# A softmax maximum per partition in a two-layer decode kernel: exp with a maximum, partial maxima joined per head, and q's copies on another engine

## The chip, the cores and the metric

The kernel runs on one core of a Trainium2 chip. A core has five engines that run side by side, each taking its own instructions in program order: TensorE (PE in the profile, its weight loads PEld), VectorE (DVE), ScalarE (ACT), GpSimd (POOL) and SyncE (SP). They meet at semaphores. Data comes from device memory (HBM) by DMA into SBUF, 128 partitions wide; matmuls write PSUM, 8 banks of 128 x 512 fp32. The metric is the device time of one execution in microseconds, lower is better. Before the change it is 1034.55 us, the median of three runs (1034.34 to 1034.6).

## The reference

Two pairs of layers on x of shape 8 x 1 x 448 in bf16. Layer A is grouped-query attention over a cache of 4096 positions, 16 query heads on 8 key/value heads of 256; layer B is a small MLP (with one position its shifted parts vanish, since they read only padding). Both pairs use the same weights and the same cache, so that the second pass reads the same K and V again.

```python
def _A_ref(x, k_cache, v_cache, wq, wo):
    q = (x @ wq).reshape(B, Sq, Hq, Dh).transpose(0, 2, 1, 3)
    k = jnp.repeat(k_cache, rep, axis=1)
    v = jnp.repeat(v_cache, rep, axis=1)
    scores = jnp.einsum("bhqd,bhkd->bhqk", q, k) * (Dh ** -0.5)
    p = jax.nn.softmax(scores, axis=-1)
    o = jnp.einsum("bhqk,bhkd->bhqd", p, v)
    return o.transpose(0, 2, 1, 3).reshape(B, Sq, Hq * Dh) @ wo

x = x + _A_ref(_layernorm(x), k_cache, v_cache, wq, wo)
x = x + _B_ref(_layernorm(x), w1, w2, w3, w4)
x = x + _A_ref(_layernorm(x), k_cache, v_cache, wq, wo)
x = x + _B_ref(_layernorm(x), w1, w2, w3, w4)
```

K and V have 8 x 8 x 4096 x 256 values each, 134 MB in bf16: 268 MB for one pass over both.

## The kernel before

**Units and tiles.** The work is cut into 64 units: pass (`ps`, 0 or 1), batch row (`b`, 0 to 7) and group pair (`gp`, 0 to 3, two key/value heads, hence four query heads). A unit has four K tiles and four V tiles of 1 MB, which lie in 17 places (`slots`, `places`) in SBUF. To save transfers, for each row 14 of the 16 tiles of group pairs 2 and 3 (called kept, and two more in part, in `rest` and in PSUM banks `store`) stay in place from pass 0 to pass 1. `free` units are those of group pairs 0 and 1.

**Order.** The list `items` fixes, ahead of time, in which order K and V tiles of which units are worked on; the loop at L1266 goes through it and issues every engine's instructions. The middle of the program is made of rounds, one per batch row. A round begins with K tiles of five units (V tiles of older units between them), and ends with the V tiles of three free units, which are read in halves (`narrow`, `halved`), while the rest of the layers for this row (wo, MLP, q of pass 1: the generator `chain`, moved on by `step`) and the kept K tiles of pass 1 go through. In that last part 14 places hold kept tiles, so that three places are left to turn over.

**Loads.** `emit_loads` issues the next transfers of the fixed order on SP's queue as soon as the program has given up a place (L920 for K, mostly two tiles at once; L931 to L937 for V). SP waits there until the place's last reader is done, and everything behind it waits with it.

**K side.** A K tile is transposed in place by DVE in 32 x 32 blocks (L1003): one instruction over 2048 words for the first tile of a pair, three (1024, 512, 512) for the second. Then PE computes the scores of the pair (`scores`, L1018), 32 matmuls of 128 x 256, with the query laid out block-diagonally in `qbd` as weights. They land in bank `sc`, on 8 of each 32 partitions: four blocks `k` of positions, in each of them four chunks by two heads. `qbd` is filled by `spread_q`: four small matmuls (L409) into `misc` and four copies by DVE (L415). ACT makes P from the scores (`exps`, L1027, one per pair): exp without a maximum, with the sum of each partition as second output in `z_t`; the profile shows an extra instruction that reads this accumulator.

**P and V.** Between the halves of the next scores, `turn_p` turns the unit's P by four matmuls with an identity (L1069) into `misc`, and ACT casts it into one of five buffers `psv` (L1076). Per V tile ACT copies the tile's part into `ptw` (L1261), and PE multiplies (`pv`, L1086) into `o`.

**After a unit.** `half` (L555) takes o out of PSUM by ACT (L546), multiplies it with R by fp32 matmuls (L592), which turns it and divides it by the sums. R is `rz` times a 0/1 pattern `fold` (L575). `rz` comes from `z_cols` (L512): DVE adds the two partial sums per partition (L518), spreads them by head with the pattern `usel` (L521), PE adds over partitions with a matrix of ones (L529), DVE takes the reciprocal (L532).

Of the kernel before, what the change touches and what calls it, by code (L numbers as in the profile page):

```python
# [17 lines left out]
def kernel(  # L18
# [79 lines left out]
    usel = consts.tile([128, 4], FP32, name="usel")  # L98
    for u in range(2):
        nc.vector.tensor_reduce(  # L100
            usel[:, 2 * u : 2 * u + 2],
            ident.rearrange("p (k q h) -> p h k q", k=4, h=2)[:, :, :, 2 * u : 2 * u + 2],
            mybir.AxisListType.XY,
            ALU.add,
        )

    parity = consts.tile([128, 2], FP32, name="parity")
    nc.vector.tensor_reduce(
        parity[:], ident.rearrange("p (m k) -> p k m", k=2), mybir.AxisListType.X, ALU.add
# [16 lines left out]
        psv_t[:, 128 * k : 128 * k + 128].rearrange("p (a n h) -> p a n h", a=4, h=2)  # L126
# [24 lines left out]
    wv = consts.tile([128, 4], FP32, name="wv")  # L151
# [3 lines left out]
    one = consts.tile([128, 1], FP32, name="one")  # L155
    nc.vector.memset(one[:], 1.0)
    ones = one[:].to_broadcast([128, 128])
# [6 lines left out]
    eps2 = consts.tile([128, 2], FP32, name="eps2")  # L164
    nc.vector.memset(eps2[:, 0:1], EPS)
    nc.vector.memset(eps2[:, 1:2], EPS * EPS / (1 + EPS))
    nhalf = consts.tile([128, 1], FP32, name="nhalf")
    nc.vector.memset(nhalf[:], -0.5)
# [66 lines left out]
    def norm(x, nb, twice, xe=None):  # L235
# [18 lines left out]
        nc.vector.tensor_mul(xx[:, 0], x, wv[:].unsqueeze(2).to_broadcast([128, 4, nb]))  # L254
# [39 lines left out]
        def power(k0, k1):  # L294
# [3 lines left out]
                nhalf[:].to_broadcast([128, (k1 - k0) * nb]),  # L298
# [3 lines left out]
        if twice and nb == 1:  # L302
            nc.vector.scalar_tensor_tensor(
                ve[:, :, 0], var.to_broadcast([128, 2]), 0.0, eps2[:], ALU.max, ALU.add
# [44 lines left out]
    def project_q(b):  # L349
# [10 lines left out]
        nc.vector.tensor_copy(OT2[:, :, HH:, b], q_ps.rearrange("p (j h) -> p j h", j=2))  # L360
        yield

    def project_rows(w_of, h0, hn, r0, r1, ps, cols=None):
# [14 lines left out]
        for j in range(2):  # L378
            nc.vector.tensor_copy(
                OT2[:, j, h0 : h0 + hn, r0:r1],  # L380
                ps[:, j * hn * nb : (j + 1) * hn * nb].rearrange("p (h b) -> p h b", b=nb),
            )

    def tail_cols(r0, r1, ps, two):
# [10 lines left out]
            parity[:].unsqueeze(2).to_broadcast([128, 2, nb]),  # L395
# [4 lines left out]
    def spread_q(b, h0, ng, qbd):  # L400
# [12 lines left out]
        for a in range(4):  # L413
            u = a // 2
            nc.vector.tensor_copy(  # L415
# [96 lines left out]
    def z_cols(zall, gps):  # L512

        np_ = len(gps)
        zm = chn.tile([128, 4, np_], FP32, tag=f"zm{np_}")
        zs_t = chn.tile([128, 2], FP32, tag="zs")
        zs = zs_t[:, 0:np_]
        nc.vector.tensor_add(  # L518
# [747 lines left out]
    for idx, it in enumerate(items):  # L1266
# [53 lines left out]
        elif kv == 0:  # L1320
# [19 lines left out]
            if c == 3 and q_begun:  # L1340
                run(q_begun.pop())
# [286 lines left out]
```

## Time and profile before

| | |
|---|---|
| median of three runs | 1034.55 us (1034.34 to 1034.6) |
| the profiled execution | 1035.43 us, its span 1033.2 us |
| mean granted TensorE clock | 0.656 |
| HBM read | 419.63 MB, 406 GB/s over the span |
| DVE: transposes of K (L1003) | 444.0 us in 384 instructions |
| PE: P times V (L1086) | 245.6 us in 3808 matmuls |
| PE: scores (L1018) | 234.8 us in 4736 matmuls |
| ACT: exp (L1027) | 95.3 us in 128 instructions, and 33.9 us for reading the accumulator |
| ACT: copies into ptw (L1261) | 52.7 us in 248 |
| DVE: q's copies (L415) | 30.8 us in 184, 61.7 us idle before them |
| DVE: reciprocals of the sums (L532) | 9.5 us in 55 |

The span is the time from the first to the last instruction; the execution's own time is 2.2 us longer. "Busy" is time in which an engine executes; waiting at a semaphore does not count. "Idle before" is an engine's idle time directly before the instructions of a group, followed by what ended most of it. The DMA share is that of the core's 16 DMA engines, which all queues share. The page's digits for 40 slices of the span show the rounds: every fourth slice or so DVE falls from 9 to 2 tenths, while DMA stays at 9 everywhere but in the last slice.

### The profile page before, as it was taken

How to read it: one execution, taken by the hardware profiler on the slowest of the kernel's cores; microseconds unless marked ns; L12 is line 12 of the kernel's file. 1: busy time of each engine (PE TensorE's matmuls, PEld its weight loads, DVE VectorE, ACT ScalarE, POOL GpSimd, SP SyncE). 2: the span in 40 equal slices, each digit the busy share in tenths (PEclk: the TensorE clock that was granted, in tenths of full speed). 3: DMA queues.
4: the chain of work that ended last, by engine and by line, in shares of the span. 5: the costliest groups of instructions: out<-in, count | busy, mean ns of one | idle time of the engine just before them, and what ended most of it. 6: DMA issues, size and time to landing. Idle time of an engine off the chain costs nothing.

```text
span 1033.2 us, 28609 instructions
## 1 busy us (share of the span) xinstructions
PE 657.3 (64%) x12707; PEld 415.6 (40%) x12707; DVE 585.8 (57%) x1213; ACT 212.7 (21%) x688; POOL 16.3 (2%) x27
## 2 busy tenths in 40 slices
PE   3154445876587557865784577558865874577775
PEld 2022222443245334533452345334533552345544
DVE  6334567159725961587249725872497259624581
ACT  1011111141214120412141214121412141214110
POOL 0000000000000000000000000000000000000000
PEclk9999855576557665566656667655565566656655
DMA  9999999999999999999999999999999999999995
GB/s 365 389 426 421 422 424 419 388 425 423 415 404 412 425 416 402 400 424 417 408 419 424 418 394 413 423 418 406 420 422 412 407 418 423 417 396 409 415 422 216
DMA packets 69290, 421.48 MB, mean 408 GB/s; under 512 B 7080, under 2 KB 12976, under 8 KB 43568
## 3 DMA queue, kind: packets, MB, share of 16 engines
q1 hardware_dynamic: 69120, 419.66, 99.1%
q8 instruction: 99, 1.62, 0.6%
q14 instruction: 23, 0.19, 0.0%
q10 hardware_dynamic: 48, 0.01, 0.0%
HBM read 419.63 MB, written 0.01 MB: 406 GB/s over the span
## 4 chain that ended last, share of the span: by engine, by line
DMA 48%; DVE 23%; PE 20%; issue 3%; SPq 3%; ACT 2%; POOL 0%; DVEq 0%; ACTq 0%
DMA places<-in_A_v_cache_dram 31%; DVE places L1003 18%; DMA places<-in_A_k_cache_dram 16%; PE sc L1018 9%; PE o L1086 5%; PE misc L180 2%; PE misc L592 2%; ACT p_n L1027 1%; DVE qbd L415 1%; DVE store L1049 1%; DMA places<-in_A_wq_dram 1%; SPq L934 1%; SPq L199 1%; PE misc L529 1%; PE misc L453 1%
## 5 line engine op out<-in xcount | busy, mean ns | idle before, releaser
L1003 DVE STREAM_TRANSPOSE places<-places 128x512 uint32<-128x512 uint32 (+2 forms) x384 | 444.0, 1213 | 44.3 <-DMA places<-in_A_k_cache_dram 43.8
L1086 PE MATMUL o<-places,ptw 128*8 128x256 bf16 x3808 | 245.6, 381 | 140.7 <-DMA places<-in_A_v_cache_dram 112.6
L1018 PE MATMUL sc<-places,qbd 128*8 128x256 bf16 (+1 forms) x4736 | 234.8, 353 | 149.2 <-DVE places L1003 148.7
L1018 PEld LDWEIGHTS <-qbd 128*8 128x8 bf16 x4736 | 122.4, 104 | 216.7 <-DVE places L1003 124.8
L1086 PEld LDWEIGHTS <-ptw 128*8 128x8 bf16 x3968 | 102.0, 101 | 205.7 <-issue 128.7
L1027 ACT ACTIVATE p_n<-sc 128x256 bf16<-128x256 f32 x128 | 95.3, 744 | 330.8 <-PE sc L1018 328.5
L1261 ACT COPY ptw<-psv 128x32 bf16<-128x32 bf16 x248 | 52.7, 227 | 179.7 <-PE o L1086 178.1
L415 DVE CAST qbd<-misc 32x16 bf16<-32x16 f32 (+1 forms) x184 | 30.8, 167 | 61.7 <-PE misc L409 59.9
L592 PE MATMUL misc<-R_t,o_t 128*128 128x4 f32 (+1 forms) x212 | 45.7, 322 | 29.1 <-DVE qbd L415 12.6
L592 PEld LDWEIGHTS misc<-R_t,o_t 128*128 128x128 f32 x212 | 41.4, 272 | 45.0 <-issue 18.7
L1076 ACT CAST psv<-misc 128x128 bf16<-128x128 f32 x64 | 17.0, 265 | 196.8 <-PE misc L1069 196.8
L532 DVE RECIPROCAL rz<-misc 128x4 f32<-128x4 f32 (+1 forms) x55 | 9.5, 172 | 80.1 <-PE misc L529 36.1
L1054 ACT COPY places<-store 128x1024 bf16<-128x1024 bf16 x40 | 40.2, 1030 | 10.6 <-PE o L1086 10.3
L529 PE MATMUL misc<-zm,one 128*128 128x4 f32 (+1 forms) x110 | 27.1, 317 | 18.4 <-DVE zm L521 16.0
L529 PEld LDWEIGHTS misc<-zm,one 128*128 128x128 f32 x110 | 22.3, 253 | 34.0 <-DVE zm L521 22.8
L180 PEld LDWEIGHTS <-w_sb 128*128 128x128 bf16 x896 | 27.8, 105 | 16.7 <-issue 16.7
L1027 ACT ACTIVATION_READ_ACCUMULATOR p_n<-sc 128x1 f32 x128 | 33.9, 265 | 0.0
L546 ACT COPY o_t<-o 128x256 f32<-128x256 f32 x53 | 19.7, 372 | 56.4 <-PE o L1086 56.3
L295 POOL TENSOR_TENSOR t<-t,nhalf 128x2 f32<-128x2 f32 (+2 forms) x18 | 12.0, 669 | 953.5 <-DVE t L316 953.5
L1049 DVE TENSOR_SCALAR store<-places 128x512 uint32<-128x512 uint32 x40 | 24.8, 673 | 0.0
L1069 PEld LDWEIGHTS <-p_n 128*128 128x128 bf16 x256 | 11.5, 104 | 29.7 <-issue 18.7
L596 DVE CAST qT<-misc 128x8 bf16<-128x8 f32 (+1 forms) x37 | 7.2, 195 | 27.1 <-PE misc L592 19.4
(157 smaller groups left out, 373.1 us busy)
## 6 DMA issues: line engine op xcount, KB each, us to landing
places<-in_A_k_cache_dram SPq DMA_DIRECT2D x79, 2048.0 KB, 15.8
places<-in_A_v_cache_dram SPq DMA_DIRECT2D x193, 512.0 KB, 7.1
places<-in_A_v_cache_dram SPq DMA_DIRECT2D x87, 1024.0 KB, 19.5
places<-in_A_k_cache_dram SPq DMA_DIRECT2D x34, 1024.0 KB, 12.3
places<-in_A_wq_dram SPq DMA_DIRECT2D x7, 768.0 KB, 10.1
rest<-in_A_v_cache_dram SPq DMA_DIRECT2D x8, 640.0 KB, 18.2
places<-in_A_v_cache_dram SPq DMA_DIRECT2D x8, 384.0 KB, 17.7
wo_sb<-in_A_wo_dram SPq DMA_DIRECT2D x1, 2688.0 KB
```

The costliest lines, as they stand in the source:

```text
L180: nc.tensor.matmul(bass.AP(out.tensor, out.offset, [out.ap[0], (1, WIDE)]), w, x.to_broadcast([128, WIDE]), start=start, stop=stop, skip_g ...
L415: nc.vector.tensor_copy(qbd[32 * a : 32 * a + 32, :, g0 : g0 + ng, a, :], qs.rearrange("p e (f g u h) -> p (e f) u g h", f=2, u=2, h=2)[:, ...
L529: nc.tensor.matmul(z_ps, ones, zm[:], start=True, stop=True)
L546: nc.scalar.copy(o_t[:], rec["ps"])
L592: nc.tensor.matmul(ot_ps[:, j], o_sb[:].rearrange("p (i j) -> p j i", j=2)[:, j], R, start=True, stop=True)
L1003: nc.vector.transpose(w, w)
L1018: nc.tensor.matmul(sc[32 * k : 32 * k + 8, 128 * (x % 2) : 128 * (x % 2 + nx)], qbd[:, ep, gp % 2].rearrange("p a h -> p (a h)"), v, start ...
L1027: nc.scalar.activation(p_sb[:, :, :, 2 * u : 2 * u + 2].rearrange("p t i x -> p x t i"), sc[:, 0:256].rearrange("p (x t i) -> p x t i", x= ...
L1049: nc.vector.tensor_single_scalar(kept_words.bitcast(U32), words.bitcast(U32), 0, op=ALU.bitwise_or)
L1054: nc.scalar.copy(words, kept_words.bitcast(BF16))
L1086: nc.tensor.matmul(o_ps[32 * q : 32 * q + 8, :], ptz[:, at : at + 8], v[:, y * Dh : (y + 1) * Dh] if v2 is None or y < PR else v2[:, (y - ...
L1261: nc.scalar.copy(ptw[:, ring_of[it], :, 6:8], psv[slot_of[it[0]]][:, it[2]])
```

## The change

**exp subtracts a maximum.** The factor -1/16 (`scale_exp` with its sign changed) is put onto q when it is copied out of PSUM (L360 and L379 of before), so that `sc` holds negated, scaled scores. Per pair of K tiles DVE takes the minimum of each partition over 256 scores (`low_max`), and ACT computes exp(-sc + low_max), with `low_max` as bias per partition. There is no accumulator output any more.

**The partial maxima are joined.** P of different partitions and of the two pairs now has different maxima. After a unit's second exp, two fp32 matmuls spread both sets of minima over the 32 used lanes onto all partitions (`both`, in `misc`); ACT takes the first set for the partitions that belong to it (`which`), DVE takes the least over lanes and sets for each head (`least`), adds the second set to `down`, subtracts `least`, and ACT computes exp(-down).

**P is rescaled.** `transpose_p` multiplies by `down` while it takes P out of PSUM: a product on DVE in place of ACT's cast. The layout of `psv` changes with it.

**The sums come from P.** `sum_p`, at the first V tile of each unit, adds the rescaled P over partitions with four bf16 matmuls, reduces on DVE and takes the reciprocal; `z_cols` and `usel` go. R is taken from it.

**When it is done.** `exps` is not issued behind its scores but put down in `exps_due`, and `flush` issues it after the transposes of the next K tile in the order and before that tile's scores, or ahead of a V or weight tile if one comes first, or at once for kept K tiles.

**q's copies** in `spread_q` move from DVE to ACT. Several small constants now share one tile `few`.

```diff
     def project_q(b):
...
-        nc.vector.tensor_copy(OT2[:, :, HH:, b], q_ps.rearrange("p (j h) -> p j h", j=2))
+        nc.vector.tensor_scalar_mul(
+            OT2[:, :, HH:, b], q_ps.rearrange("p (j h) -> p j h", j=2), -scale_exp
+        )
...
     def spread_q(b, h0, ng, qbd):
...
-            nc.vector.tensor_copy(
+            nc.scalar.copy(
                 qbd[32 * a : 32 * a + 32, :, g0 : g0 + ng, a, :],
                 qs.rearrange("p e (f g u h) -> p (e f) u g h", f=2, u=2, h=2)[:, :, u],
             )
...
-    def z_cols(zall, gps):
...
+    def sum_p(who, p_of_unit):
+
+        z_ps = misc[:, 0:32]
+        for t in range(4):
+            nc.tensor.matmul(
+                z_ps, oneb.to_broadcast([128, 128]), p_of_unit[:, t], start=(t == 0), stop=(t == 3)
+            )
+        rz_of[who] = rz_free.pop(0)
+        nc.vector.tensor_reduce(
+            rz_t[:, rz_of[who]],
+            z_ps.rearrange("p (n m) -> p n m", n=4),
+            mybir.AxisListType.X,
+            ALU.add,
+        )
+        nc.vector.reciprocal(rz_t[:, rz_of[who]], rz_t[:, rz_of[who]])
...
-    def exps(p_sb, zall, gp, u):
+    def exps(p_sb, u):
+
+        nc.vector.tensor_reduce(low_max[:, u : u + 1], sc[:, 0:256], mybir.AxisListType.X, ALU.min)
         nc.scalar.activation(
             p_sb[:, :, :, 2 * u : 2 * u + 2].rearrange("p t i x -> p x t i"),
             sc[:, 0:256].rearrange("p (x t i) -> p x t i", x=2, t=4),
             ACT.Exp,
-            scale=scale_exp,
-            accum_out=zall[:, u, gp : gp + 1],
-        )
+            bias=low_max[:, u : u + 1],
+            scale=-1.0,
+        )
+        if u == 0:
+            return
+        both = misc[:, 0:64]
+        for k in range(2):
+            nc.tensor.matmul(
+                both[:, 32 * k : 32 * k + 32],
+                low_max[:, k : k + 1].to_broadcast([128, 128]),
+                lanes[:],
+                start=True,
+                stop=True,
+            )
+        nc.scalar.mul(down, both[:, 0:32], which[:, 0:1])
+        nc.vector.tensor_reduce(
+            least,
+            both.rearrange("p (u n m) -> p n u m", u=2, n=4),
+            mybir.AxisListType.XY,
+            ALU.min,
+        )
+        nc.vector.scalar_tensor_tensor(
+            down, both[:, 32:64], which[:, 1:2], down, ALU.mult, ALU.add
+        )
+        by_head = down.rearrange("p (n m) -> p n m", n=4)
+        nc.vector.tensor_tensor(
+            by_head, by_head, least.unsqueeze(2).to_broadcast([128, 4, 8]), ALU.subtract
+        )
+        nc.scalar.activation(down, down, ACT.Exp, scale=-1.0)
+
+    exps_due = []
+
+    def flush():
+        while exps_due:
+            exps(*exps_due.pop(0))
...
     def transpose_p(p_sb, p_to):
...
-        nc.scalar.copy(p_to, pt_ps.rearrange("p t k (a h) -> p a (t k) h", a=4))
+        nc.vector.tensor_tensor(
+            p_to, pt_ps, down.unsqueeze(1).to_broadcast([128, 4, 32]), ALU.mult
+        )
...
         final = (ps, b) == (1, Bn - 1)
+        if kv:
+            flush()
...
             if not kept_now:
                 transpose_k(slot, late(it) and c % 2 == 0)
+            flush()
...
             if c % 2 == 1:
-                exps(p_of[n], st["z"], gp, c // 2)
+                exps_due.append((p_of[n], c // 2))
+                if kept_now:
+                    flush()
...
             spread_p(it)
+            if it == v_first[n]:
+                sum_p((ps, b, gp), psv[slot_of[n]])
```

In `half`, R (one product per group pair) is now formed from `take_rz` before the generator waits for the unit's last V tile, and the steps that `z_cols` took there fall away.

## The prediction

> **What bounds the kernel now.** I read the page first: engines, DMA queues and the chain of waits.
>
> ```profile
> PE 657.3 (64%) x12707; PEld 415.6 (40%) x12707; DVE 585.8 (57%) x1213; ACT 212.7 (21%) x688; POOL 16.3 (2%) x27
> q1 hardware_dynamic: 69120, 419.66, 99.1%
> DMA 48%; DVE 23%; PE 20%; issue 3%; SPq 3%; ACT 2%; POOL 0%; DVEq 0%; ACTq 0%
> ```
>
> The transfers hardly pause (99.1% for 419.66 MB), and no engine is near its limit on average. Yet DVE has 23% of the chain, so I looked at stages. Seven rounds of some 103 us are alike (their K transposes start at 223, 324, 429, 531, 634, 740 and 839 us); a first (122 to 185) and a last one (940 to 1010) differ. Busy times by window of those two and of both halves of one round (PE, PEld, DVE, ACT, POOL, granted clock, DMA share, GB/s):
>
> ```profile
> 122.00:185.00 63.00, 31.32 (x536) 18.11 (x539) 42.41 (x55) 9.87 (x34) 0.00 (x0) 0.53 1.01 420
> 223.00:279.00 56.00, 33.99 (x680) 20.28 (x674) 51.08 (x67) 14.86 (x41) 0.00 (x0) 0.65 1.01 421
> 279.00:324.00 45.00, 35.65 (x651) 22.29 (x644) 9.85 (x55) 8.83 (x35) 1.25 (x2) 0.58 1.02 403
> 940.00:1010.00 70.00, 48.89 (x1078) 34.89 (x1063) 45.72 (x97) 16.20 (x49) 1.99 (x2) 0.61 1.01 419
> ```
>
> From 223 to 279 DVE is busy 51.1 of 56 us: the **K stretch**, 20 K tiles. From 279 to 324 it is nearly idle: the **V stretch**. The DVE timeline shows how little the K stretch waits (start, length, in brackets the wait before):
>
> ```profile
> 254.68 7.19 DVE L1003 STREAM_TRANSPOSE places<-places 128x1024 uint32<-128x1024 uint32 x7
> ...
> 264.61 2.31 DVE L1003 STREAM_TRANSPOSE places<-places 128x2048 uint32<-128x2048 uint32 x1 [0.69 <-DMA places<-in_A_k_cache_dram]
> ...
> 269.69 9.13 DVE L1003 STREAM_TRANSPOSE places<-places 128x2048 uint32<-128x2048 uint32 x8 [0.38 <-DMA places<-in_A_k_cache_dram]
> ```
>
> So DVE and DMA run level here, and what DVE loses beyond a cushion, the transfers lose: a place is free only after transpose and scores. The cushion is read from DMA issues by window, in this order 281 to 284, 286 to 300 and 436.5 to 437.6 us (KB, us to landing):
>
> ```profile
> places<-in_A_v_cache_dram SPq DMA_DIRECT2D x2, 512.0 KB, 9.5
> ...
> places<-in_A_v_cache_dram SPq DMA_DIRECT2D x11, 512.0 KB, 6.9
> ...
> places<-in_A_k_cache_dram SPq DMA_DIRECT2D x1, 2048.0 KB, 8.6
> ```
>
> The third is the quickest K pair that I found: 2.1 MB at 420 GB/s are 5.0 us, so 3.6 us are fixed. A V half (1.25 us) would land in 4.9 us on an empty queue; at the end of the K stretch it takes 9.5. The queue therefore holds about 4.5 us that DVE may be late.
>
> **The change, part by part.** The rows for the prices (busy us, mean ns of one | idle before):
>
> ```profile
> L1003 DVE STREAM_TRANSPOSE places<-places 128x2048 uint32<-128x2048 uint32 x96 | 220.4, 2296 | 44.3 <-DMA places<-in_A_k_cache_dram 43.8
> L1003 DVE STREAM_TRANSPOSE places<-places 128x512 uint32<-128x512 uint32 x192 | 121.2, 670 | 0.0
> L1027 ACT ACTIVATE p_n<-sc 128x256 bf16<-128x256 f32 x128 | 95.3, 744 | 330.8 <-PE sc L1018 328.5 <-PE misc L409 2.0
> L1261 ACT COPY ptw<-psv 128x32 bf16<-128x32 bf16 x248 | 52.7, 227 | 179.7 <-PE o L1086 178.1 <-PE misc L409 1.1
> L546 ACT COPY o_t<-o 128x256 f32<-128x256 f32 x53 | 19.7, 372 | 56.4 <-PE o L1086 56.3
> L415 DVE CAST qbd<-misc 32x16 bf16<-32x16 f32 x112 | 17.8, 159 | 34.6 <-PE misc L409 33.5
> L532 DVE RECIPROCAL rz<-misc 128x4 f32<-128x4 f32 x46 | 7.9, 173 | 80.1 <-PE misc L529 36.1 <-ACT ptw L1261 28.6 <-ACT o_t L546 15.4
> L1049 DVE TENSOR_SCALAR sc<-places 128x256 uint32<-128x256 uint32 x8 | 3.4, 428 | 7.5 <-ACT p_n L1027 7.5
> L264 DVE TENSOR_REDUCE t<-misc 128x2 f32<-128x8 f32 x16 | 2.7, 167 | 10.6 <-PE misc L260 10.6
> ```
>
> A unit is four K tiles, transposed in two pairs; five units make a K stretch. DVE gets per unit:
> (a) two minima over 256 scores. No such row exists. Below, the reduction of 8 (0.167); above, 512 words (L1049, 0.673). Nearest is 256 words, 0.428; I take 0.40 each, 0.80.
> (b) the wait in the second flush. DVE's next instruction (least) waits for ACT's product into down, which stands behind the exp of the same scores: 0.744 + 0.227 = 0.97 by L1027 and L1261; if the exp without accumulator were as quick as L546, 0.372 + 0.227 = 0.60; with hand-overs up to 1.2. PE's two joining matmuls run beside it (before, from zm's end to the reciprocal at 214.53, one took 0.47). I take 0.95, L1027 being the same function on the same layout. Queued behind it are the next transposes, and for those PE and SP wait.
> (c) least, the sum into down and the subtraction: three small ones at 0.17 to 0.19, 0.53.
> (d) the product into psv, 0.30 (L379 casts 64 elements in 0.220, L1049 256 in 0.428), and 0.10 of waiting for PE: from the first of the three transpose pieces on, half the scores (16 matmuls took 1.02 at 237.94) and P's four matmuls (0.29 at 238.89) against two pieces of 0.670.
> Together 2.68, five times 13.4 us.
> (e) In the changed program's order six of the stretch's ten flushes come directly after the pieces whose scores they need: PE's two halves and P take 2.0 to 2.3, the remaining pieces 1.34, psv's product comes between; wait 0 to 1.0, I take 0.7: 4.2. The other four come after the next tile's 2.296 and wait for nothing.
> (f) Two sums of P (reduction, reciprocal, 0.35, and a wait of 0 to 0.6, say 0.4 for PE's four matmuls): 1.5.
> (g) The first transposes now stand behind the last kept unit's join: 0.40 + 0.95 + 0.53 + 0.75 for its P sum is 2.6. Gone there are a q spread (0.77 at 220.99) and a z column with its wait (1.2). Scores of the second kept pair may overwrite sc only after an exp that starts a minimum later (0.45), and PE's join of the other kept unit stands before them (0.8). Together 2.0, between 0.7 and 3.
> (h) Removed: two q spreads in the stretch, 4 x 0.159 = 0.65 each, 1.3; three z columns (L518, L521, L532, 0.16 + 0.16 + 0.17), 1.5.
> Net: 13.4 + 4.2 + 1.5 + 2.0 - 2.8 = **18.3 us of DVE per round**. Taken up: waits for K 1.1, about 1.0 of waits for ACT (263.76 and 280.39), the cushion 4.5. Left: 18.3 - 6.6 = 11.7, seven times 82 us. The first round has waits for K of 10.8 us (4.35, 0.68, 4.74, 0.68, 0.39): 18.3 - 10.8 - 4.5 = 3 us. The last has 24 idle DVE us of 70: nothing.
>
> At nothing I put, under DMA's cover: before 122 us, where DVE is half idle; P's sums and joins in the V stretch (DVE 9.85 of 45; uncovered 0.75 and 1.9 per unit); on ACT q's copies (184 x about 0.23 = 42), the products and the exps of down (128 x 0.23 = 29), against 33.9 for accumulator reads and 17.0 for psv's casts that go. ACT is busy 14.9 of 56. PE's additions are 256 small and 128 joining matmuls. SP's transfers and their order are unchanged.
>
> The sum is made against the profiled run, 1035.4 (span 1033.2 and 2.2 around it), 0.9 above the median of 1034.55: 1035.4 + 85 = 1120.4, less 0.9 is **1120 us**.
>
> [...]
>
> **The rivals.** *The waits overlap.* If (b), (d) and (e) wait for nothing, since PE and ACT are done in time, 5 x 1.63 + 0.7 + 0.7 - 2.8 = 6.8 are left, and 6.6 take that up: 1036; with a quarter of the 12 us of waits, 1056. For it: DMA 99%, ACT 21%. Against it: DVE takes its instructions in order, and least waits for an exp that cannot start before the minimum.
> *The convoy is longer.* In the V stretch ACT's q copies (0.9 per spread) and the kept units' joins stand before the ptw copies that PE needs; a V half has 1.25 us. With 2 us per kept unit, two a round, it is 8 x 4 = 32 more: 1152; with (a) to (g) at their upper ends, 5 x 3.75 + 6 + 2 + 3 - 2.8 - 4.1 = 23 per round, 1207.
> *Faster.* DVE loses q's 30.8 us with 61.7 us of waits, z's columns with 80.1 before the reciprocals; the chain at the end of the V stretch loses a matmul, a reciprocal and a product. If the V stretch then ran at 421 instead of 403 GB/s, 45 x 18/421 = 1.9 us, eight times 15: 1020. It decides only if DVE's growth per round stays under the 6.6; against that, the waits removed lie mostly where DVE idles.
>
> **How the numbers follow.** Forecast 0.61 (1055 to 1170), overlapped 0.18 (1036 to 1055, of it 0.05 within 0.2%, about 2 us and what can be told from no change), longer convoy 0.13 (above 1150), faster 0.08. With all prices low, 5 x 1.73 + 0.7 + 0.7 - 2.8 - 6.6 = 0.7 per round, 1040; all high 1207. Range for 8 in 10: 1050 to 1170. Faster 0.08, same 0.05, slower 0.87.
>
> **What would show it.** Right: K stretches longer by 9 to 14 us, rounds by as much; DVE's waits before least mostly on ACT at 0.6 to 1.2 us; DMA share under 0.95 toward the end of the K stretch; DVE's sum near 655. Wrong: DMA still at 99%; minima under 0.25 us; the loss in the V stretch.

## The result

| | before | after |
|---|---|---|
| median (runs) | 1034.57 us (four, 1034.34 to 1035.28) | 1151.39 us (four, 1148.84 to 1153.23) |
| ratio | | 1.1124, 95% interval 1.1111 to 1.1137 |
| span of the profiled execution | 1033.2 us | 1151.1 us |
| granted clock, mean | 0.656 | 0.591 |

The forecast was 1120 us, in a range of 1050 to 1170. The change costs 117 us. Lines move by some 33 with the change: transposes are L1036 now, scores L1051, the minimum L1061, exp L1062, the joining matmuls L1073, ACT's product L1080, least L1081, the sum and the subtraction L1087 and L1091, exp of down L1094, psv's product L1142, the sum of P L549 and L553, q's copies L448.

The page of after, engines, queue and chain of waits:

```profile
PE 732.3 (64%) x13109; PEld 472.2 (41%) x13109; DVE 654.0 (57%) x1388; ACT 263.8 (23%) x808; POOL 16.3 (1%) x27
q1 hardware_dynamic: 69120, 419.66, 90.8%
DVE 36%; PE 27%; DMA 24%; ACT 6%; issue 4%; SPq 2%; POOL 0%; DVEq 0%; ACTq 0%
```

The same bytes now fill 90.8% of the span instead of 99.1%; in the chain DMA has 24% where it had 48%. No engine is busy for more than two thirds of the span; the time has to be looked for in what they wait for.

The starts of the K stretches tell where the time is lost. The first begins at 231.0 us (before: 223.1), the last at 1064.2 (946.3), and from there to the end it is 86.9 us in both kernels. So the first round adds 7.8, seven rounds add 110.1, 15.7 each, and the last adds nothing: 117.9 in all, the difference of the spans. One round by windows (the columns are those of the windows shown before: PE, PEld, DVE, ACT, POOL, clock, DMA share, GB/s), the K stretch and the V stretch behind it:

```profile
231.00:297.00 66.00, 38.86 (x700) 23.36 (x696) 55.99 (x82) 16.98 (x43) 0.00 (x0) 0.60 0.88 356
297.00:349.00 52.00, 38.32 (x684) 25.37 (x680) 12.24 (x61) 12.37 (x47) 1.25 (x2) 0.60 0.94 367
```

The K stretch was 56 us long with DVE busy for 51.1; now it is 66 with 56.0, so half of its growth is DVE work and half is waiting. The V stretch has grown as well, from 45 to 52 us, with DVE busy for a quarter of it. Ten-microsecond windows of the same round show where the transfers run dry:

```profile
270.00:280.00 10.00, 8.14 (x108) 4.69 (x107) 7.83 (x14) 1.70 (x5) 0.00 (x0) 0.50 0.69 266
280.00:290.00 10.00, 3.93 (x72) 2.62 (x68) 8.86 (x13) 2.10 (x4) 0.00 (x0) 0.67 1.01 414
290.00:300.00 10.00, 5.55 (x76) 3.13 (x77) 7.47 (x13) 2.09 (x4) 0.00 (x0) 0.50 0.94 379
300.00:310.00 10.00, 8.48 (x166) 5.33 (x166) 3.09 (x16) 2.19 (x10) 0.69 (x1) 0.76 0.68 233
```

In the middle of the K stretch the share falls to 0.7; toward its end it is back at 1.01 and 0.94, and it falls once more right behind it, where no K tiles are transposed.

The groups of instructions by shape (busy us, mean ns of one | idle before, releasers):

```profile
L1062 ACT ACTIVATE p_n<-sc,few 128x256 bf16<-128x256 f32 x128 | 105.9, 827 | 498.4 <-DVE few L1061 409.2 <-DVE rz L553 44.0 <-DVE R_t L601 25.1
L1061 DVE TENSOR_REDUCE few<-sc 128x1 f32<-128x256 f32 x128 | 53.0, 414 | 96.2 <-PE sc L1051 80.1 <-PE misc L442 16.1
L1142 DVE TENSOR_TENSOR psv<-misc,down 128x128 bf16<-128x128 f32 x64 | 18.3, 286 | 30.4 <-PE misc L1135 27.9 <-ACT down L1094 2.4
L1087 DVE SCALAR_TENSOR_TENSOR down<-misc,few,down 128x32 f32<-128x32 f32 x64 | 15.5, 242 | 0.0
L1081 DVE TENSOR_REDUCE few<-misc 128x4 f32<-128x64 f32 x64 | 14.3, 224 | 71.6 <-ACT down L1080 71.6
L1091 DVE TENSOR_TENSOR down<-down,few 128x32 f32<-128x32 f32 x64 | 12.3, 191 | 2.2
L553 DVE TENSOR_REDUCE rz<-misc 128x4 f32<-128x32 f32 x64 | 12.1, 189 | 42.2 <-PE misc L549 42.2
L629 DVE CAST qT<-misc 128x8 bf16<-128x8 f32 x28 | 5.3, 189 | 57.2 <-PE misc L625 33.9 <-ACT qbd L448 23.3
```

All of these are DVE's but the first; the last is the cast of o after it was turned (L596 before), under the name that its target shares with q. The row to look at is least (L1081): 71.6 us of waiting in 64 instructions, 1.12 each, every one of them for ACT's product. One such join in the K stretch, first DVE's and then ACT's timeline:

```profile
258.39 0.39 DVE L1061 TENSOR_REDUCE few<-sc 128x1 f32<-128x256 f32 x1
259.82 0.22 DVE L1081 TENSOR_REDUCE few<-misc 128x4 f32<-128x64 f32 x1 [1.05 <-ACT down L1080]
259.97 0.24 DVE L1087 SCALAR_TENSOR_TENSOR down<-misc,few,down 128x32 f32<-128x32 f32 x1
260.24 0.19 DVE L1091 TENSOR_TENSOR down<-down,few 128x32 f32<-128x32 f32 x1
260.35 2.42 DVE L1036 STREAM_TRANSPOSE places<-places 128x1024 uint32<-128x1024 uint32 x3
```

```profile
258.81 0.83 ACT L1062 ACTIVATE p_n<-sc,few 128x256 bf16<-128x256 f32 x1 [4.12 <-DVE few L1061]
259.50 0.29 ACT L1080 ACTIVATE down<-misc,few 128x32 f32<-128x32 f32 x1
```

From the start of the minimum to the next transposes 1.96 us pass (258.39 to 260.35), of which DVE works for about 0.9. ACT is idle for 4.12 us, then does exp and the product one after the other, and only then may DVE go on.

At the end of the V stretch, ahead of the first transposes of the next round, DVE's timeline reads so:

```profile
340.59 0.19 DVE L629 CAST qT<-misc 128x8 bf16<-128x8 f32 x1 [1.54 <-PE misc L625]
...
345.82 0.19 DVE L629 CAST qT<-misc 128x8 bf16<-128x8 f32 x1 [4.66 <-ACT qbd L448]
345.90 0.41 DVE L1061 TENSOR_REDUCE few<-sc 128x1 f32<-128x256 f32 x1
347.48 0.23 DVE L1081 TENSOR_REDUCE few<-misc 128x4 f32<-128x64 f32 x1 [1.17 <-ACT down L1080]
...
348.25 0.19 DVE L553 TENSOR_REDUCE rz<-misc 128x4 f32<-128x32 f32 x1 [0.16 <-PE misc L549]
348.48 0.18 DVE L559 RECIPROCAL rz<-rz 128x4 f32<-128x4 f32 x1
348.94 2.31 DVE L1036 STREAM_TRANSPOSE places<-places 128x2048 uint32<-128x2048 uint32 x1 [0.28 <-issue]
```

DVE waits most of the time, but its first transpose stands in order behind the cast of o, the second kept unit's minimum, its join and a sum of P. From PE's first scores of the kept units to that transpose it was 14.0 us in this round before (310.5 to 324.4), and is 20.6 now (328.3 to 348.9).

### The profile page after: what moved, and what is told of

It is laid out like the page before. It is cut to its first block, busy times and chain, and to the rows that moved or that the text cites. A ratio compares the mean times of both kernels' runs of the same rounds, so it can differ in the third digit from the quotient of the medians.

```text
span 1151.1 us, 29813 instructions
## 1 busy us (share of the span) xinstructions
PE 732.3 (64%) x13109; PEld 472.2 (41%) x13109; DVE 654.0 (57%) x1388; ACT 263.8 (23%) x808; POOL 16.3 (1%) x27
## 3 DMA queue, kind: packets, MB, share of 16 engines
q1 hardware_dynamic: 69120, 419.66, 90.8%
## 4 chain that ended last, share of the span: by engine, by line
DVE 36%; PE 27%; DMA 24%; ACT 6%; issue 4%; SPq 2%; POOL 0%; DVEq 0%; ACTq 0%
DVE places L1036 26%; DMA places<-in_A_v_cache_dram 16%; PE sc L1051 12%; DMA places<-in_A_k_cache_dram 9%; PE o L1154 6%; ACT p_n L1062 4%; DVE few L1061 3%; PE misc L210 2%; PE misc L625 2%; DVE store L1116 2%; DVE few L1081 1%; ACT down L1080 1%; SPq L967 1%; SPq L229 1%; DVE down L1087 1%
## 5 line engine op out<-in xcount | busy, mean ns | idle before, releaser
L1036 DVE STREAM_TRANSPOSE places<-places 128x512 uint32<-128x512 uint32 (+2 forms) x384 | 445.7, 1212 | 17.8 <-DMA places<-in_A_k_cache_dram 15.0
L1051 PE MATMUL sc<-places,qbd 128*8 128x256 bf16 (+1 forms) x4736 | 246.0, 362 | 191.3 <-DVE places L1036 174.3
L1051 PEld LDWEIGHTS <-qbd 128*8 128x8 bf16 x4736 | 128.0, 106 | 263.8 <-issue 111.7
L1062 ACT ACTIVATE p_n<-sc,few 128x256 bf16<-128x256 f32 x128 | 105.9, 827 | 498.4 <-DVE few L1061 409.2
L1061 DVE TENSOR_REDUCE few<-sc 128x1 f32<-128x256 f32 x128 | 53.0, 414 | 96.2 <-PE sc L1051 80.1
L1073 PE MATMUL misc<-lanes,few 128*128 128x32 f32 x256 | 74.2, 393 | 30.4 <-DVE few L1061 17.1
L1073 PEld LDWEIGHTS misc<-lanes,few 128*128 128x128 f32 x256 | 59.3, 296 | 56.6 <-DVE few L1061 24.6
L1081 DVE TENSOR_REDUCE few<-misc 128x4 f32<-128x64 f32 x64 | 14.3, 224 | 71.6 <-ACT down L1080 71.6
L448 ACT CAST qbd<-misc 32x16 bf16<-32x16 f32 (+1 forms) x184 | 31.1, 169 | 53.9 <-PE misc L442 35.8
L629 DVE CAST qT<-misc 128x8 bf16<-128x8 f32 (+1 forms) x37 | 7.1, 191 | 57.2 <-PE misc L625 33.9
L553 DVE TENSOR_REDUCE rz<-misc 128x4 f32<-128x32 f32 x64 | 12.1, 189 | 42.2 <-PE misc L549 42.2
L1142 DVE TENSOR_TENSOR psv<-misc,down 128x128 bf16<-128x128 f32 x64 | 18.3, 286 | 30.4 <-PE misc L1135 27.9
L549 PE MATMUL misc<-psv,few 128*128 128x32 bf16 x256 | 17.9, 190 | 23.5 <-DVE down L1087 16.9
L549 PEld LDWEIGHTS <-few 128*128 128x128 bf16 x256 | 13.1, 106 | 34.7 <-DVE down L1087 19.6
```

The lines of the kernel that those rows point to most:

```text
L448: nc.scalar.copy(qbd[32 * a : 32 * a + 32, :, g0 : g0 + ng, a, :], qs.rearrange("p e (f g u h) -> p (e f) u g h", f=2, u=2, h=2)[:, :, u],)
L549: nc.tensor.matmul(z_ps, oneb.to_broadcast([128, 128]), p_of_unit[:, t], start=(t == 0), stop=(t == 3))
L1036: nc.vector.transpose(w, w)
L1051: nc.tensor.matmul(sc[32 * k : 32 * k + 8, 128 * (x % 2) : 128 * (x % 2 + nx)], qbd[:, ep, gp % 2].rearrange("p a h -> p (a h)"), v, start ...
L1061: nc.vector.tensor_reduce(low_max[:, u : u + 1], sc[:, 0:256], mybir.AxisListType.X, ALU.min)
L1062: nc.scalar.activation(p_sb[:, :, :, 2 * u : 2 * u + 2].rearrange("p t i x -> p x t i"), sc[:, 0:256].rearrange("p (x t i) -> p x t i", x= ...
```

## The experiments

Each kernel is the changed one with one edit, and was timed beside the kernel before (medians there 1035.02, 1034.08, 1035.76 and 1035.23 us). For each the table gives the mean of seven rounds of two stretches: K, from the first transpose to the end of the last, and the gap from there to the next first transpose. Both are read from the transposes' own times.

| kernel | median us | ratio to before, 95% | K us | gap us | DMA share |
|---|---|---|---|---|---|
| before | 1034.57 | | 56.1 | 47.2 | 99.1% |
| after | 1151.39 | 1.1124 (1.1111 to 1.1137) | 67.0 | 52.0 | 90.8% |
| q's copies on DVE | 1169.03 | 1.1292 (1.1269 to 1.1315) | 68.9 | 51.9 | 89.5% |
| no join | 1050.53 | 1.0142 (1.0115 to 1.0168) | 59.7 | 45.3 | 98.6% |
| no minima, no join | 1036.39 | 1.0015 (1.0006 to 1.0025) | 59.2 | 43.9 | 99.1% |
| late flush | 1123.1 | 1.0858 (1.083 to 1.0885) | 66.9 | 47.8 | 93.1% |
| product on DVE | 1145.21 | 1.1083 (1.1059 to 1.1106) | 67.1 | 51.0 | 91.3% |
| minima twice | 1201.0 | 1.1619 (1.1601 to 1.1636) | 71.2 | 53.8 | 87.1% |
| split join | 1128.52 | 1.0909 (1.0886 to 1.0932) | 65.9 | 49.9 | 92.4% |
| late flush, split join | 1097.13 | 1.0598 (1.058 to 1.0617) | 62.7 | 48.8 | 95.1% |
| the same, sums of P later | 1105.04 | 1.0677 (1.0632 to 1.0723) | 65.0 | 47.1 | 94.7% |
| no join of the kept units | 1110.13 | 1.0705 (1.066 to 1.075) | 67.2 | 46.4 | 93.9% |
| least ahead of the product | 1155.41 | 1.1166 (1.1133 to 1.1199) | 67.5 | 52.1 | 90.4% |
| late flush, split join, none for kept units | 1083.55 | 1.0458 (1.0435 to 1.0481) | 62.1 | 47.8 | 95.7% |

**q's copies back on DVE.** One part undone.

```diff
-            nc.scalar.copy(
+            nc.vector.tensor_copy(
                 qbd[32 * a : 32 * a + 32, :, g0 : g0 + ng, a, :],
```

> The changed kernel with q's four copies per spread back on DVE. Theory A (DVE sets the pace of the K stretch, what it does there is paid): two spreads per round at 0.65 us and a wait for PE each, so 1.3 to 3 us more per round, 9 to 21 in all: 1160 to 1172. Theory B (the copies on ACT are what lengthens the kept part at the end of the V stretch, since in the changed trace a join waits 0.77 us for them and o's transposition stands behind them): 1 to 2 us less per round there, 7 to 14 in all, which cancels A or beats it: 1140 to 1155.

Measured 1169.03: 17.6 us slower than after, for 30.9 us more of DVE work (684.9 busy against 654.0). Moving q's copies helps the changed kernel; the copies on ACT are not what it loses by. The K stretch bears it (+1.9 us a round), the gap does not move, though DVE's casts of o no longer wait for ACT there (33.4 us before 28 casts, 33.3 of them for PE; in after 57.2, 23.3 of them for ACT).

**No join.** exp with its minimum stays, the matmuls, the product, least, sum, subtraction and exp of down are left out, and down is 1.

```diff
+    nc.vector.memset(down, 1.0)
...
-        if u == 0:
+        if u < 2:
             return
```

> The changed kernel without the join: the two fp32 matmuls, the product, least, the sum and the subtraction and the second exp are left out, and down stays 1, so that P keeps the maximum of its own partition and its pair (another result than the reference's). Theory A (a wait of 1.1 us before least and 0.66 us of small DVE work in each unit, in a K stretch and in the kept part alike): 5 x 1.8 = 9 us per round in the K stretch, and most of the 6.7 us by which the kept part has grown: 11 to 14 per round, 80 to 100 in all, so 1050 to 1070. Theory B (the time goes to the minima and to their waits for the scores, and the join runs beside them): at most 4 us per round, 1120 or more.

Measured 1050.53: the join alone is 101 of the 117 us. K is 7.3 us a round shorter, the gap 6.7.

**No minima either.** The minimum and the bias of exp are left out as well. What is left of the change is psv's product on DVE, the sums from P, the later place of exp and q's move.

```diff
-        nc.vector.tensor_reduce(low_max[:, u : u + 1], sc[:, 0:256], mybir.AxisListType.X, ALU.min)
...
-            bias=low_max[:, u : u + 1],
...
-        if u == 0:
+        if u < 2:
             return
```

> As the kernel without the join, and without the minima: exp has no bias (another result than the reference's where scores are large, the same here up to rounding). What is left of the change is the sum from P, the product into psv on DVE, the late issue of exp and q's copies on ACT. Theory A (minima cost 0.41 us each and wait for scores six times per K stretch): 10 x 0.41 + 4 us per round less than without the join, so what is left costs 0 to 2 us per round: 1035 to 1048. Theory B (DVE's product into psv and the sums of P, for which DVE stops until PE has turned P, are a large part): 1060 or more.

Measured 1036.39, over ten runs, 1.5 us above before. With the join gone the minima are worth 14 us, and all the rest of the change together 1.5. Here DMA binds again: its queue fills 99.1% of the span, as before.

**Minima twice.** The same minimum is taken a second time into the same place: DVE work alone, with no new wait for another engine.

```diff
+        nc.vector.tensor_reduce(low_max[:, u : u + 1], sc[:, 0:256], mybir.AxisListType.X, ALU.min)
         nc.vector.tensor_reduce(low_max[:, u : u + 1], sc[:, 0:256], mybir.AxisListType.X, ALU.min)
```

> The changed kernel with every minimum taken twice (the same instruction once more directly behind it): 128 more DVE instructions of 0.41 us. Theory A (DVE sets the pace in the K stretch and in the kept part, so that added DVE work is paid in full): ten per round in the K stretch and four in the kept part, 5.8 us per round, 40 to 48 in all: 1191 to 1200. Theory B (DVE is mostly waiting for PE there, and work on it fills its waits): the second minimum falls into the wait before least only for half of them; under 20 us: below 1171.

Measured 1201.0: 50 us more for 54.3 us of work (708.4 against 654.0). In the changed kernel DVE's time is paid nearly in full; the minima, 53 us of work with the waits before them, cost 14 on the kernel without a join, where the transfers still fill 98.6% of the span. A price per instruction alone does not tell the cost; the slack at that point does.

**Product on DVE.** ACT's product into down, for which least waits, becomes a DVE instruction behind least.

```diff
-        nc.scalar.mul(down, both[:, 0:32], which[:, 0:1])
         nc.vector.tensor_reduce(
             least,
...
         )
+        nc.vector.tensor_scalar_mul(down, both[:, 0:32], which[:, 0:1])
```

> The changed kernel with the join's first product (the first set of minima times its partitions, into down) on DVE, behind least, in place of ACT: least then waits for PE's two joining matmuls alone, no longer for ACT's exp of 0.83 us and product of 0.29 us. Theory A (the wait before least is ACT's, 1.12 us a unit, and DVE pays it): the wait falls to 0.5 to 0.7, DVE gets 0.2 more per unit, so 0.2 to 0.4 less for each of some seven units per round that count, 10 to 22 us in all: 1129 to 1141. Theory B (PE's matmuls end as late as ACT's product): the wait stays at 1.0 and DVE's product adds 0.2 per unit, 8 to 13 us: 1159 to 1165.

Measured 1145.21, between the theories. The group of least in this kernel:

```profile
L1080 DVE TENSOR_REDUCE few<-misc 128x4 f32<-128x64 f32 x64 | 14.4, 225 | 51.0 <-PE misc L1073 49.9 <-ACT p_n L1062 1.1
```

The wait is 51.0 instead of 71.6, and another engine ends it: without ACT, PE's two joining matmuls are done 0.80 us after the minimum. DVE pays 15.5 us for the product: 20.6 us less of waiting and 15.5 more of work, 5 in all, and the time fell by 6. The wait for PE had been hidden beneath the one for ACT.

**Late flush.** The exp is issued after the next K tile's transposes even where a V or weight tile, or a kept tile, would have called it earlier; only a V tile whose own unit's P is still to be turned calls it.

```diff
-        if kv:
+        if kv and n in p_of:
             flush()
...
-                if kept_now:
-                    flush()
```

> The changed kernel, all of its arithmetic, but a due exp is no longer issued ahead of every V tile, nor at once for kept tiles: only ahead of the next K tile's scores (behind its transposes, where it has any), or ahead of a V tile of a unit whose P is still to be turned. Theory A (six of ten flushes in a K stretch wait for scores that have just begun, and the first transposes of a round stand behind the last kept unit's join): 4 us less per round in the K stretch and 4 to 5 in the kept part, 50 to 65 in all: 1085 to 1100. Theory B (the work itself is what is paid, and a wait that is avoided here comes back at the product into psv, which then waits for the later exp): less than 15 us, 1136 or more.

Measured 1123.1, 28 us less than after, which is neither forecast. Three of its groups:

```profile
L1061 DVE TENSOR_REDUCE few<-sc 128x1 f32<-128x256 f32 x128 | 50.4, 394 | 44.8 <-PE sc L1051 44.8
L1081 DVE TENSOR_REDUCE few<-misc 128x4 f32<-128x64 f32 x64 | 14.4, 225 | 68.3 <-ACT down L1080 68.3
L553 DVE TENSOR_REDUCE rz<-misc 128x4 f32<-128x32 f32 x64 | 12.3, 192 | 64.1 <-PE misc L549 64.1
```

The minima wait for 44.8 us, not 96.2, but the sums of P for 64.1 where it was 42.2: part of a wait that is taken away comes back at the next place where DVE needs PE. The K stretch stays at 66.9; the gain is in the gap (52.0 to 47.8).

**Split join.** The matmuls and ACT's product stay in flush; least, sum, subtraction and exp of down are put off until P is turned, so that transposes lie between. For that the sum of P uses other columns of `misc`.

```diff
         nc.scalar.mul(down, both[:, 0:32], which[:, 0:1])
+        joins_due.append(both)
+
+    def join():
+        if not joins_due:
+            return
+        both = joins_due.pop(0)
         nc.vector.tensor_reduce(
             least,
...
     def turn_p():
+        join()
         n = next(iter(p_of))
```

> The changed kernel with the join in two parts alone, exps issued as in the changed kernel. Theory A: 5 x 1.1 us less per K stretch, and less in the kept part than with the late flush, since the first transposes still stand behind the minimum of the last kept scores but not behind its join: 7 to 8 per round, 50 to 65 in all: 1086 to 1101. Theory B (the wait comes back at the product into psv): over 1135.

Measured 1128.52, between the theories. Two groups:

```profile
L1089 DVE TENSOR_REDUCE few<-misc 128x4 f32<-128x64 f32 x64 | 12.7, 198 | 10.6 <-ACT down L1080 9.1 <-PE misc L625 1.5
L553 DVE TENSOR_REDUCE rz<-misc 128x4 f32<-128x32 f32 x64 | 12.2, 190 | 77.5 <-PE misc L549 77.5
```

The wait before least is nearly gone (10.6 of 71.6), and 35 of these 61 us are back before the sums of P (77.5 instead of 42.2). The time fell by 23 us, close to the remaining 26.

**Late flush and split join together.** The two edits above in one.

> The kernel with the late flush, and the join in two parts: the two matmuls and ACT's product are issued with the second exp as before, but DVE's part (least, sum, subtraction) and the second exp only when P is turned, behind the next tile's transposes; the sum of P uses other columns of its bank. All arithmetic is kept. Theory A (the wait of 1.1 us before least is paid once per unit): it disappears; against the late flush alone 5 x 1.1 us less per K stretch and 2 in the kept part, 7 per round, 45 to 60 in all: 1063 to 1080. Theory B (DVE then waits as long at the product into psv, for the exp that comes later, or at the sums): within 15 us of the late flush alone, 1108 to 1125.

Measured 1097.13, between the theories: 26 us less than the late flush alone and 54 less than after. It is the best version here that still does all that the change does, and it is 6% above before. Its groups:

```profile
L1061 DVE TENSOR_REDUCE few<-sc 128x1 f32<-128x256 f32 x128 | 50.5, 394 | 43.5 <-PE sc L1051 43.5
L1089 DVE TENSOR_REDUCE few<-misc 128x4 f32<-128x64 f32 x64 | 13.0, 203 | 28.7 <-ACT down L1080 18.4 <-PE misc L625 8.6 <-PE misc L486 1.7
L553 DVE TENSOR_REDUCE rz<-misc 128x4 f32<-128x32 f32 x64 | 12.3, 192 | 64.2 <-PE misc L549 64.2
```

With transposes between, 28.7 us of waiting are left before least, and K is 62.7 us. The order of the instructions alone is worth nearly half of the loss.

**The same, with the sums of P at the second V tile.** The 64.2 us before the sums are the largest wait left.

```diff
+    v_second = {n: [it for it in v_items if it[0] == n][1] for n in v_first}
...
-            if it == v_first[n]:
+            if it == (v_first[n] if final else v_second[n]):
```

> The kernel with late flush and split join, and the sum of P issued at a unit's second V tile in place of its first (but for the last row). All arithmetic is kept. Theory A (in that kernel DVE waits 1.0 us before each reduction of the sum, 64 us in all, since PE still has scores and o's transposition in front of it, and the first transposes of a round stand behind such a wait): two sums per K stretch and one ahead of it, 3 to 4 us per round, 20 to 30 in all: 1067 to 1077. Theory B (the V tile itself is what DVE and PE wait for there, and the wait moves on with the sum): within 8 us, 1089 to 1100.

Measured 1105.04, a miss of both theories: no gain, 8 us worse. The wait before the sums falls from 64.2 to 45.3 us and the gap from 48.8 to 47.1, but the K stretch grows from 62.7 to 65.0; why it does is not shown. A large wait in the list need not be what the time goes by.

**No join of the kept units.** In the second pass the kept units' P is not rescaled and its maxima are not joined; everything else is as in after.

```diff
-        if u == 0:
+        if u == 0 or alone_p:
             return
...
-        transpose_p(p_of.pop(n), psv[slot_of[n]])
+        plain_p = tasks[n][0] == 1 and tasks[n][2] in keep
+        transpose_p(p_of.pop(n), psv[slot_of[n]], *([one] if plain_p else []))
```

> The changed kernel without the join for the kept units of the second pass alone (two per row, which are scored in the kept part at the end of the V stretch; their P keeps the maximum of its partition and pair); the five units of the K stretch keep theirs. Theory A (the join costs about as much in the kept part as in the K stretch: of the 14.2 us per round that leaving out all joins gave, 6.9 lay between the last transposes of a round and the first of the next): 5 to 7 us less per round, 38 to 55 in all: 1096 to 1113. Theory B (the space between the transposes is longer because the K stretch ends late and its last unit's join stands ahead of its V tiles): less than 15 us, 1136 or more.

Measured 1110.13, 41 us less than after. K stays at 67.2, and the gap falls by 5.6 us, to 46.4. So 16 of the 64 joins carry 41 of the 101 us, and they carry it at the end of the V stretch, ahead of the next round's first transposes.

**The same in the best version.** Late flush and split join, and no joins of the kept units in the second pass (both edits above).

> Late flush and split join, and the kept units' joins of the second pass left out (their P is not rescaled). Theory A, the kept units' joins still cost where DVE's part stands behind other work: half or more of the 41 us that they cost in the changed kernel goes, 1065 to 1080 us, and the gap between K stretches falls from 48.8 to under 46 us. Theory B, with the join split they are hidden, and the gap is set by the casts of o and the sums of P: 1088 to 1098 us, the gap above 47.5.

Measured 1083.55, 13.6 us less than with those joins, between the theories: split, they still cost, but a third of what they did, and the gap only falls from 48.8 to 47.8 us.

**Least ahead of the product.** Least needs nothing of ACT's product: both read what PE wrote into `misc`. Here their order is turned round.

```diff
-        nc.scalar.mul(down, both[:, 0:32], which[:, 0:1])
         nc.vector.tensor_reduce(
             least,
...
         )
+        nc.scalar.mul(down, both[:, 0:32], which[:, 0:1])
```

> Least is issued ahead of ACT's product; nothing is left out. Both only read what PE's joining matmuls wrote into the bank misc, and neither reads the other's result. Theory A, two engines' reads of one bank are kept in program order: least waits for PE alone, about 0.80 us (51 us in all, as with the product on DVE), the product then begins only when least is done, and the sum behind it waits for ACT for 0.3 us or more (20 us in all). From the minimum to the transposes it stays at about 2 us, and the time at 1145 to 1165 us. Theory B, reads are not ordered: least waits for PE about 0.80 us, the product runs beside it, the sum waits for next to nothing, and the time falls by 6 to 16 us, to 1135 to 1145.

Measured 1155.41. DVE's two groups and ACT's product:

```profile
L1080 DVE TENSOR_REDUCE few<-misc 128x4 f32<-128x64 f32 x64 | 14.4, 225 | 51.2 <-PE misc L1073 51.2
L1087 DVE SCALAR_TENSOR_TENSOR down<-misc,few,down 128x32 f32<-128x32 f32 x64 | 16.1, 251 | 23.7 <-ACT down L1086 23.7
L1086 ACT ACTIVATE down<-misc,few 128x32 f32<-128x32 f32 x64 | 18.4, 288 | 11.7 <-DVE few L1080 9.8
```

Theory A: now least waits for PE alone, the product for least (9.8 us), and the sum for the product (23.7). The wait before least in the changed kernel is thus no need of its data: two engines read the same bank, and in this program the one that comes second waits (least 71.6 us there, the product 9.8 us here). The two share one more tile, `few`: the product reads `which` there, and least writes there. One join of this kernel, DVE's line and ACT's, shows that a shared `few` alone makes no wait:

```profile
259.06 0.23 DVE L1080 TENSOR_REDUCE few<-misc 128x4 f32<-128x64 f32 x1 [0.72 <-PE misc L1073]
...
258.36 0.83 ACT L1062 ACTIVATE p_n<-sc,few 128x256 bf16<-128x256 f32 x1 [4.17 <-DVE few L1061]
```

exp reads its bias from `few` until 259.19, and least, which writes into other columns of `few`, starts at 259.06; it starts ahead of exp's end in 62 of the 64 joins.

## Why the prediction was right, and what it mis-sized

The mechanism held: the join makes DVE wait for ACT in the middle of the transposes (4.3 us in the four joins of the K stretch of the round shown, 71.6 in all 64), DVE's order passes that on to the K places (SP's waits for transposes ahead of the loads of K are 203.5 us, and 160.5 before), and the transfers run dry (90.8% of the span against 99.1%). No join, and 101 of 117 us are gone; neither minima nor join, and the kernel is as fast as before but for 1.5 us. DVE's sum is 654.0 (655 was named), the K stretch grew by 10.9 us (9 to 14 named), and the waits before least are ACT's and 1.12 us on average (0.6 to 1.2). Of the other signs that it named, the DMA share does fall, to 0.7, but in the middle of the K stretch and not toward its end; the round grew by 15.7 us and not by 9 to 14; and 4.8 of these lie in the gap, where a loss was to speak against the forecast.

The size was 32 us low (85 against 117), and the parts that made it:

- (a) the minimum: 0.414 us in after (0.394 with the late flush), 0.40 taken.
- (b) the wait before least: 1.12 us, 0.95 taken, within the upper end of 1.2. exp is 0.827 instead of 0.744, the product 0.287 instead of 0.227. That least waits for the product at all is the bank they share, by the kernel with the two turned round; it adds little: the sum needs the product itself, which ends 1.40 us after the start of the minimum in the join shown (258.39 to 259.79), and the sum starts at 1.58, so that without the bank some 0.15 us of a join would go, an estimate. exp's 83 ns more came with its bias of one value per partition. That it lost its accumulator output in the same edit does not blur this: in the kernel without minima, where it has neither, exp took 744 ns, as before.
- (c) 0.66 us (224 + 242 + 191 ns), 0.53 taken.
- (d) the product into psv: 0.286 and a mean wait of 0.47 (30.4 us in 64), where 0.30 and 0.10 were taken. In the K stretch proper it waits for less (0.7 us in five).
- (e) and (f), oversized. DVE's groups in the K stretch of the round shown above, 231 to 297 us:

```profile
L1061 DVE TENSOR_REDUCE few<-sc 128x1 f32<-128x256 f32 x9 | 3.7, 406 | 2.9 <-PE sc L1051 2.9
L1142 DVE TENSOR_TENSOR psv<-misc,down 128x128 bf16<-128x128 f32 x5 | 1.4, 276 | 0.7 <-PE misc L1135 0.7
L1081 DVE TENSOR_REDUCE few<-misc 128x4 f32<-128x64 f32 x4 | 0.9, 224 | 4.3 <-ACT down L1080 4.3
L553 DVE TENSOR_REDUCE rz<-misc 128x4 f32<-128x32 f32 x2 | 0.4, 186 | 0.2 <-PE misc L549 0.2
```

The minima wait for PE's scores for 2.9 us here (4.2 taken), the sums for 0.2 (0.8). There are nine minima and four joins, not ten and five: in all seven rounds the last unit's second minimum and join stand behind the last transpose (297.38 to 299.52 us in this round), so that some 1.9 us which the forecast put into the K stretch (0.40, 0.95 and 0.53) fall into the gap. Of the waits taken up it counted about 1.0 for ACT, where the two rows that it names have 1.89 and 0.98, the second of them behind the stretch. With that, the forecast for the K stretch, 18.3 less the 2.0 of (g) and the 2.1 of waits that were taken up, 14.2 us, was 3.3 above the 10.9 measured.

- The step that failed is the rest of the round. The forecast had the V stretch give 2.5 us back: 2.0 more by (g), the kept units ahead of the first transposes, and 4.5 less by the cushion of DMA's queue. Measured, the gap grew by 4.8 (52.0 against 47.2). Term (g) was the mis-sized one: the joins of the two kept units alone are 5.6 us there, by the kernel without them, and (g) had 2.0, with 3 as its upper end. It had one kept unit's join in full and of the other only 0.45 and 0.8 us. It missed that between two kept units DVE, ACT and PE pass the work to and fro, one instruction at a time: in the timeline above the casts of o and the joins wait 1.54, 4.66 and 1.17 us. The cushion was not all there either: by PE's timeline up to the kept units' scores, the round shown gained 1.8 us on before in the narrow V tiles (22.5 against 24.3), and lost 1.9 ahead of them, where the last unit's join stands.
- The first round, 3 us forecast, lost 7.8. The last, none forecast, lost none. DVE is busy for 49.5 of the 70 us from 1064 there (44.8 of the 70 from 946 before), so that its idle time may have taken up the growth, as the forecast had it; no run tests that.

Per round that is 3.3 too much in K and 7.3 too little in the gap, 4.0 in all (15.7 against 11.7); seven times that, and 4.8 in the first round, are the 33 us by which the span's growth (117.9) passed the forecast. The two errors have opposite signs, so that the total came out nearer than its parts; that much is luck.

Of the rivals, the overlapping waits are ruled out by the wait before least, 71.6 us, and by the 50 us that a second minimum costs. The faster kernel would have needed DVE's growth to stay within its slack: the kernel without minima and join does so, and even that is not faster. The longer convoy was right about a place: what the V stretch loses is the joins of kept units, as it said (it had 4 us a round for them, and 5.6 were there). Its 1152 us is the measured time but for 1 us, and between 1150 and 1170 its band and the forecast's overlap, so that the time alone does not choose between them. That it is met so closely is luck: its sum per round, 11.7 + 4, is the 15.7 measured, with 3.3 too much in the K stretch and 3.3 too little in the gap. It was wrong about q's copies on ACT as a net loss: taking them back made the kernel 17.6 us slower.

What stays open: the late flush and the split join each gained less than the waits at which they were aimed. Those waits reappear before the sums of P and at the casts of o: added up over DVE's minima, least, sums, casts of o and products into psv, the waits fell by 31 and 22 us, and the time by 28 and 23. Which of the waits that are left then sets the time is not shown. Nor is it settled what the join's work on PE costs by itself: its fp32 matmuls keep PE busy for 74.2 us in all, and no run leaves out these alone. It is open as well what keeps the gap at 47.8 us in the best version when even the kept units' joins are gone; there 65.3 us of waiting before the sums of P and 72.9 before the casts of o are left, but putting the sums off did not help.

## What to carry to other kernels

Price a new dependency between engines by the round trip that it puts into the order of the engine that sets the pace (here 1.1 us of waiting for an instruction of 0.2), and put independent work of that engine between the two ends: done for the minima and the join together, that was worth 54 of 117 us here. Look for the same round trip in the stretch where the engine seems idle, directly ahead of the work that starts the next round: there 16 of 64 joins cost 41 of 101 us. And test what a share of busy time is worth by doubling one piece of work: some 54 us of minima cost 14 with slack and 50 without.

## What the runs showed of the hardware

- exp with a bias per partition took 827 ns for 128 x 256 (744 without, with an accumulator output before and with none in the kernel without minima), and the accumulator's own 265 ns instruction is gone. ACT's sum rose all the same, from 212.7 to 263.8 us, while it is busy for 23% of the span: it was the wait for ACT, not its sum, that cost.
- The granted clock was lower in after (0.591 against 0.656), and the score matmuls over 256 columns took 387 ns against 382, those of P times V 386 against 381, about 1%; the 1280 score matmuls over 128 columns took 297 against 273, 9%. All scores together are 245.9 us against 234.8. The late flush does the same work at a clock of 0.627, and the kernel without the join has 0.633; no kernel was run to separate the clock's part.
- A reduction of 4 x 16 values per partition out of PSUM took 224 ns, little above one of 4 x 8 (189 ns), and 198 to 203 in the versions with the join split; the join's other two DVE instructions took 242 and 191 ns.
- In the joins of after and of the kernel with least ahead of the product, the later of ACT's and DVE's two reads of the bank `misc` waited for the earlier: least 71.6 us for the product in the one, the product 9.8 us for least in the other. These two read columns that overlap. The casts of o and ACT's copies of q read different columns, and the casts still wait for the copies: in the round shown PE's matmuls for the cast end at 345.02, the copies run from 345.05 to 345.79, and the cast starts at 345.82. By the profile's names `misc` is the only tile that both use. So 0.8 of the 4.66 us before that cast are the copies', and the rest PE's; of the 23.3 us that are put down to the copies in all, most may be PE's likewise. Spreading small results over banks was not tried.
